# Attention softmax maxima turned by VectorE through DRAM instead of by TensorE, and two copies moved between engines

## The chip, the cores and the metric

The kernel runs on one core of a Trainium2 chip. The core has a matrix engine (PE in the profile, with a separate row PEld for its weight loads), a vector engine (VectorE, DVE), a scalar engine (ScalarE, ACT), GpSimd (POOL) and SyncE (SP), which here only issues transfers; ScalarE can issue transfers too. The engines work side by side and wait for each other by semaphores. PSUM is the memory that the matrix engine writes, in eight banks of 128 partitions by 512 fp32 numbers; SBUF is the large memory on chip; DRAM is outside. The metric is the time of one execution on the device in microseconds (us).

## The reference

One transformer block in fp32: layer norm, attention with 32 heads of width 20, output projection and residual, then layer norm, a gated feed-forward part and a second residual. S is 2048 tokens, D is 640, F is 1728.

```python
def _A_ref(x, wqkv, wo):
    qkv = (x @ wqkv).reshape(B, S, 3, H, Dh).transpose(2, 0, 3, 1, 4)
    q, k, v = qkv[0], qkv[1], qkv[2]
    scores = jnp.einsum("bhqd,bhkd->bhqk", q, k) * (Dh ** -0.5)
    p = _softmax(scores, axis=-1)
    o = jnp.einsum("bhqk,bhkd->bhqd", p, v)
    return o.transpose(0, 2, 1, 3).reshape(B, S, D) @ wo

def _B_ref(x, w_gate, w_up, w_down):
    return (_silu(x @ w_gate) * (x @ w_up)) @ w_down

h = x + _A_ref(_layernorm(x), A_wqkv, A_wo)
out = h + _B_ref(_layernorm(h), B_w_gate, B_w_up, B_w_down)
```

The softmax subtracts the maximum of each row of scores, one maximum for each head and query. That maximum is what the change is about.

## The kernel before

The kernel goes through three stages. In the first (up to the first score product, at 322.8 us) the inputs are normed and projected to queries, keys and values, and most maxima of the first units are worked out beside this. The second is attention proper (the last score product starts at 1468.4 us). The third is the projection of the attention's outputs and the feed-forward part.

**Units and steps.** Attention is cut into 32 units `u`: eight groups of four heads, and in each group four blocks of 512 queries (`g, c = divmod(u, 4)`). A unit takes 16 steps `kt`, one tile of 128 keys each, so there are 512 steps. In each step PE makes four score products (`scores`, L1182, its matmul is L1187), one for each head, keys by queries, into four PSUM banks that take turns. ScalarE takes the exponential out of the bank (L1193). The probabilities are then weighed with the values: `weigh` (L1195) makes four small matmuls for each step into one accumulator bank, `acc`, and it works on the step two back. There is only one accumulator, so a new unit's first weighing must wait until the last unit's sums have been copied out of it.

**Maxima.** The queries in SBUF, `q_stk`, hold for each pair of heads 60 rows of data and two rows more. These two rows (the *query rows* from here on) hold minus the maximum, split in a high and a low part so that no precision is lost in the matrix engine's rounded format (`F32R`); against rows of ones in the keys, the score product then comes out with the maximum taken away. So a unit's scores cannot begin before its query rows are written. The maxima come from products of their own with queries on the partitions: `max_one` (L240) makes one matmul of 128 queries by 512 keys in one of three PSUM banks (`ps_max`), and VectorE takes the maximum along the row (L250). Three of these go into every step, always for a later unit. When the last of a unit is done, `next_max` calls `max_all`: VectorE takes the maximum over the four blocks of keys and negates it, which leaves `neg`, 128 queries by 16 columns. Now the numbers stand along the partitions, but the query rows want them along a row, so they have to be turned. `max_finish` (L261) does this two steps later (`closing`): PE transposes them into one of the score banks, `split` (L87) rounds them to the high part on ScalarE and takes the rest on VectorE, and four transfers on SP bring them into the query rows.

**The order of a step** is written out by hand: `ORDER` holds the strings `"WsSmmSsM"` and `"WSsMMsSm"` for even and odd steps (`s`, `S` a score product, `m`, `M` a product for maxima, `W` the weighing with all that hangs on it: the turn of finished maxima, one task of the preparation of weights). Where no maxima remain, it is `"sSsSW"`. As the maxima run ahead evenly, the turn comes at different distances from the unit that needs it. In the kernel before, in units 2, 4, 6 and so on to 30 the turn stands nine steps ahead of the unit's first score, in units 5, 9, 13 and so on to 29 fifteen steps, and in units 1, 3, 7, 11, 15, 19, 23, 27 and 31 only four.

**What else runs beside it.** At the end of each unit `row_sums` (L1205) copies the whole accumulator with one ScalarE instruction (128x512) to SBUF and gathers the sums of the exponentials from it with small transfers; `reciprocals` writes one over them to DRAM (`r_d`), `spread` reads them back to all partitions (`rb`), and `store_o` multiplies and stores. `prepare_weights` (L988) works on the feed-forward part's weights, one task per step: a load on SP, sums on GpSimd, splits into high and low parts on GpSimd, and stores on SP (`store` in each task issues what the task before finished). `split_wo` (L883) splits the five pieces of the output weights late in the stage, the rounding on ScalarE and the rest on GpSimd. All transfers named here but the gathered sums of the last unit are issued by SP, in the order of the program; one that waits holds up those behind it. The same is true of each engine's own instructions.

Of the kernel before, what the change touches and what calls it, by code (L numbers as in the profile page):

```python
# [9 lines left out]
F32 = mybir.dt.float32  # L10
BF16 = mybir.dt.bfloat16
F32R = mybir.dt.float32r
I32 = mybir.dt.int32
AF = mybir.ActivationFunctionType
ALU = mybir.AluOpType
AX = mybir.AxisListType

P = 128
# [7 lines left out]
CH = 512  # L26
# [18 lines left out]
def tile_block(ctx: ExitStack, tc: tile.TileContext, x, wqkv, wo, wg, wu, wd, out):  # L45
# [10 lines left out]
    v_d = dram.tile([S, NG, VG], F32, name="v_d")  # L56
    o_d = dram.tile([D, S], F32, name="o_d")
    r_d = dram.tile([H, S], F32, name="r_d")
    z_d = [dram.tile([P, 2 * ND * CH], F32R, name=f"z_d{c}") for c in range(2)]
    t_d = [dram.tile([P, 8 * CH], F32R, name=f"t_d{i}") for i in range(2)]  # L60
    w_d = [dram.tile([P, 8, 4 * P], F32R, name=f"w_d{f}") for f in range(NF)]
# [191 lines left out]

    def max_all(u):

        ends[u] = stk.tile([P, G * TPC], F32, name="neg", tag="neg", bufs=2)
        nc.vector.tensor_reduce(
            ends[u], mxs[u].rearrange("p b h t k -> p (b h t) k"), axis=AX.X, op=ALU.max, negate=True
        )

    def max_finish(u):  # L261

        m = (ps_one if u else ps_max)()[: G * TPC, :P]
        nc.tensor.transpose(m, ends.pop(u), ident)
        parts = stk.tile([G * TPC, 2, P], F32R, name="m2", tag="m2", bufs=1)
        split(m, parts[:, 0], parts[:, 1], nc.vector)
        for b in range(2):
            for i in range(2):
                row = b * ROW + NPART + i
                first = b * 2 * TPC  # L270
                nc.sync.dma_start(
                    queries[u][row : row + 1].bitcast(F32).rearrange(
                        "r j (t p) -> r (j t) p", t=TPC
                    ),
                    parts[first : first + 2 * TPC, i, :].bitcast(F32),
                )
# [604 lines left out]
        nc.sync.dma_start(wo_raw[k], wo[k * P : (k + 1) * P, :])  # L881

    def split_wo(k):  # L883
        split(wo_raw.pop(k), wo_hi[:, k, :], wo_lo[:, k, :], nc.gpsimd)

    def projection(c, ps_of):

# [316 lines left out]

    def row_sums(acc, *queues):  # L1205
        o = pc.tile([P, CH], F32, name="o", bufs=1)
        nc.scalar.activation(o, acc, AF.Copy)  # L1207
        r = pc.tile([P, 16], F32, name="r")
        for j in range(G):
            queues[j % len(queues)].dma_start(  # L1210
                r[32 * j : 32 * j + 32, :],
                o[32 * j + DH : 32 * j + DH + 1, :].rearrange("r (p f) -> r p f", p=32),
            )
        return o, r
# [28 lines left out]
    def next_max(b):  # L1243
        if singles[b]:
            a = singles[b].pop(0)
            max_one(*a)
            left[a[0]] -= 1
            if left[a[0]] == 0:
                max_all(a[0])
                closing[a[0]] = now[0] + 2  # L1250

    def weigh_next():
        u, kt, probs = todo.pop(0)
# [9 lines left out]
    for u in range(NU):  # L1263
# [4 lines left out]
        for kt in range(NT):  # L1268
# [5 lines left out]
            for op in order:  # L1274
                if op in "mM":
                    next_max(int(op == "M"))
                elif op in "sS":
                    scores(u, kt, heads[op == "S"].pop(0), probs)
                else:
                    if len(todo) == 2:  # L1280
                        weigh_next()
                    for v in ready:
                        max_finish(v)
                    if extra:
                        extra.pop(0)()
                    if preparing and u and kt not in (3, 4):
                        preparing.pop(0)()
                    if now[0] == (NU - NC) * NT + 8:
                        unit_ring, last_ring = weight_rings()
                        unit_ring.fill()  # L1290
                        last_ring.fill()
# [603 lines left out]
```

## Time and profile before

| | |
|---|---|
| median of three runs | 2038.93 us (2038.71 to 2042.29) |
| the profiled execution | 2038.82 us, span of its trace 2037.0 us |
| PE busy | 2012.7 us, 99% of the span |
| PEld busy (overlaps PE) | 1249.9 us, 61% |
| VectorE busy | 1607.9 us, 79% |
| ScalarE busy | 1445.2 us, 71% |
| GpSimd busy | 774.1 us, 38% |
| exponentials, L1193 | 2048 on ScalarE, 614 ns each |
| maxima in attention, L250 | 1472 on VectorE, 684 ns each |
| score products, L1187 | 2048 on PE, 450 ns each |
| weighing, L1197 | 4096 on PE in the profile's count, 604 ns each |
| mean granted clock of PE | 0.999 |

The span begins with the first instruction and ends with the last; the execution's own time is a little longer. The ends of PE's matmuls are modelled and they overlap in its pipeline, so its busy share of 99% does not say that it is at its limit everywhere. In rows of the order of time the first number is the start in us from the span's beginning, the second the duration, then come the engine, the line of the kernel, the operation and the tile it writes and reads; a row with `x3` stands for three instructions in a run, and the brackets tell the idle time before it and what ended it. `SPq` rows are transfers as SP issues them, with the time it takes to issue.

### The profile page before, as it was taken

The page shows a single profiled execution, that of the slowest core. Times are in us where ns is not written, and L with a number is a line of the kernel's source. Part 1 is how long each engine was busy: PE and PEld are TensorE (multiplying, and loading weights), DVE is VectorE, ACT ScalarE, POOL GpSimd, SP SyncE. Part 2 cuts the span into 40 slices and gives each one's busy share as a digit, 9 for nine tenths or more (in the row PEclk, how much of TensorE's full clock was granted, in tenths as well). Part 3 has the DMA queues.
Part 4 walks back from the last instruction along what each step waited for, and adds up shares of the span by engine and source line. Part 5 has one row for each costly group of instructions (what it writes and reads, how often), then busy time and mean ns, then how long its engine had stood idle before and what let it go on. Part 6 is the DMA issues. An engine that isn't in the chain of part 4 may idle for free.

```text
span 2037.0 us, 40049 instructions
## 1 busy us (share of the span) xinstructions
PE 2012.7 (99%) x14322; PEld 1249.9 (61%) x14322; DVE 1607.9 (79%) x2826; ACT 1445.2 (71%) x2855; POOL 774.1 (38%) x1103
## 2 busy tenths in 40 slices
PE   8999999999999999999999999999999999999999
PEld 6989995343334333334333433345598888888888
DVE  5677778888888888888888888886378666676677
ACT  4677778999999999999999999987633222211221
POOL 6464423334342444352400011011146454754555
PEclk9999999999999999999999999999999999999999
DMA  7877563452634534435512131311158654974542
GB/s 244 255 244 260 175 206 89 116 161 79 187 104 124 166 115 143 149 127 176 156 46 79 27 94 44 92 62 55 33 184 302 220 192 157 344 273 158 202 150 94
DMA packets 194062, 310.01 MB, mean 152 GB/s; under 512 B 47760, under 2 KB 82576, under 8 KB 192840
## 3 DMA queue, kind: packets, MB, share of 16 engines
q1 hardware_dynamic: 187272, 283.85, 43.0%
q0 software_dynamic: 6496, 23.60, 4.0%
q8 instruction: 114, 1.87, 0.4%
q14 instruction: 84, 0.69, 0.1%
q10 hardware_dynamic: 96, 0.00, 0.0%
HBM read 207.75 MB, written 98.83 MB: 151 GB/s over the span
## 4 chain that ended last, share of the span: by engine, by line
PE 87%; DMA 3%; DVE 1%; issue 1%; POOL 1%; ACT 1%; SPq 1%; ACTq 0%; DVEq 0%; POOLq 0%
PE acc L1197 24%; PE ps_one L1187 16%; PE ps_a L1358 15%; PE ps_max L244 12%; PE ps_b L1452 8%; PE ps_one L568 6%; PE ps_max L211 2%; PE ps_max L918 2%; PE ps_b L918 1%; DMA units<-w_d 1%; DMA halves<-j_d 0%; DMA h<-in_A_x 0%; PE ps_max L953 0%; DVE tmp L1573 0%; ACT o L1207 0%
## 5 line engine op out<-in xcount | busy, mean ns | idle before, releaser
L1193 ACT ACTIVATE probs<-ps_one 128x512 f32<-128x512 f32 x2048 | 1056.7, 614 | 62.3 <-PE ps_one L1187 37.6
L250 DVE TENSOR_REDUCE mx<-ps_max 128x1 f32<-128x512 f32 x1472 | 926.2, 684 | 106.9 <-PE ps_one L1187 75.6
L1187 PE MATMUL ps_one<-q_stk,k_stk 62*128 62x512 f32 x2048 | 586.0, 450 | 2.8 <-DVE m L89 1.8
L1197 PE MATMUL acc<-probs,v_stk 128*32 128x512 f32 x4096 | 545.2, 604 | 0.0
L1187 PEld LDWEIGHTS ps_one<-q_stk,k_stk 62*128 62x128 f32 x2048 | 251.5, 184 | 432.7 <-ACT probs L1193 398.3
L244 PE MATMUL ps_max<-k_stk,q_stk 60*128 60x512 f32 x1472 | 381.2, 425 | 0.0
L244 PEld LDWEIGHTS ps_max<-k_stk,q_stk 60*128 60x128 f32 x1472 | 271.6, 186 | 24.1 <-DVE mx L250 0.9
L1573 DVE TENSOR_TENSOR tmp<-ps_a,tmp 128x512 f32<-128x512 f32 x208 | 141.2, 689 | 120.3 <-PE ps_a L1358 94.6
L233 DVE TENSOR_REDUCE mx<-ps_max 128x2 f32<-128x512 f32 x288 | 180.6, 685 | 66.5 <-PE ps_max L211 63.4
L1232 POOL TENSOR_TENSOR o<-o,rb 128x512 f32<-128x512 f32 x31 | 39.9, 1287 | 413.3 <-DMA q_stk<-q_d 241.5
L1197 PEld LDWEIGHTS acc<-probs,v_stk 128*32 128x32 f32 x4096 | 80.6, 108 | 174.8 <-issue 166.2
L223 ACT ACTIVATE ps_max<-ps_max 128x512 f32<-128x512 f32 x288 | 151.7, 583 | 47.5 <-PE ps_max L211 44.7
L1452 PE MATMUL ps_b<-halves,yp 128*128 128x320 f32 x1032 | 179.3, 308 | 2.0 <-DMA halves<-j_d 1.2
L1452 PEld LDWEIGHTS ps_b<-halves,yp 128*128 128x128 f32 x1032 | 165.1, 188 | 18.6 <-POOL yp L89 1.5
L1358 PE MATMUL ps_a<-t,units 128*128 128x512 f32 x624 | 162.6, 396 | 0.0
L1358 PE MATMUL ps_a<-z,units 128*128 128x512 f32 x516 | 133.9, 394 | 0.0
L89 POOL TENSOR_TENSOR yp<-y,yp 128x256 fp32r<-128x256 f32 x96 | 60.4, 629 | 188.2 <-ACT yp L88 188.2
L1358 PEld LDWEIGHTS ps_a<-t,units 128*128 128x128 f32 x624 | 112.6, 188 | 18.9 <-ACT tmp L1586 0.3
L1457 DVE TENSOR_TENSOR h<-ps_b,h 128x320 f32<-128x320 f32 x248 | 110.0, 481 | 6.9 <-PE ps_b L1452 5.4
L568 PE MATMUL ps_one<-z_hi,w_lo 64*128 64x512 f32 x380 | 113.7, 395 | 0.0
L568 PE MATMUL ps_one<-z_hi,w_hi 64*128 64x512 f32 x380 | 113.1, 396 | 0.0
L568 PE MATMUL ps_one<-z_lo,w_hi 64*128 64x512 f32 x380 | 111.7, 393 | 0.0
(211 smaller groups left out, 2643.3 us busy)
## 6 DMA issues: line engine op xcount, KB each, us to landing
units<-w_d SPq DMA_DIRECT2D x186, 256.0 KB
w_d<-stage SPq DMA_DIRECT2D x106, 256.0 KB
halves<-j_d SPq DMA_DIRECT2D x70, 320.0 KB
j_d<-stage SPq DMA_DIRECT2D x42, 320.0 KB
k_stk<-k_d SPq DMA_DIRECT2D x64, 160.0 KB
q_stk<-q_d SPq DMA_DIRECT2D x64, 160.0 KB
raw<-k_d SPq DMA_DIRECT2D x62, 160.0 KB
raw<-q_d SPq DMA_DIRECT2D x54, 160.0 KB
```

Of the source, the lines that this page charges most:

```text
L223: nc.scalar.activation(ps, ps, AF.Relu)
L233: nc.vector.tensor_reduce(mx[:, b, :, t, kc], ps.rearrange("p (j n) -> p j n", j=2), axis=AX.X, op=ALU.max,)
L244: nc.tensor.matmul(ps, queries[u][rows, pair, t * P : (t + 1) * P], keys[u // NC][rows, pair, kc * CH : (kc + 1) * CH], start=True, stop=True,
L250: nc.vector.tensor_reduce(mxs[u][:, b, pair, t, kc : kc + 1], ps, axis=AX.X, op=ALU.max)
L568: nc.tensor.matmul(ps, a[rows], b[rows], start=(i == n == 0), stop=(i == 1 and n == last), skip_group_check=True,)
L1187: nc.tensor.matmul(ps, keys[u // NC][rows, p, kt * P : (kt + 1) * P], queries[u][rows, p, :], start=True, stop=True,)
L1193: nc.scalar.activation(probs[p][:, b, :], ps, AF.Exp, scale=scale)
L1197: nc.tensor.matmul(acc[32 * j : 32 * j + 32, :], values[u // NC][:, kt, j * VW : j * VW + 32], probs[j // 2][:, j % 2, :], start=(kt == 0) ...
L1358: nc.tensor.matmul(ps.rearrange("p (t n) -> p t n", t=TPC), w[k][:, i], z[k][:, :, j], start=(first and m == 0), stop=(last and m == len(n ...
L1452: nc.tensor.matmul(ps, a, b, start=(n == 0), stop=(n == len(pairs) - 1))
L1457: nc.vector.tensor_tensor(out=h, in0=ps, in1=h, op=ALU.add)
L1573: add = lambda out, ps, x: nc.vector.tensor_tensor(out=out, in0=ps, in1=x, op=ALU.add)
```

## The change

Four things are changed.

1. *Maxima.* For every unit but the first, `max_all` now also splits the negated maxima into high and low parts, with two GpSimd instructions (a rounding copy and a subtraction), into one tile of 128 by 32. A new function `max_turn` takes the place of `max_finish` (which stays for unit 0): VectorE's own transpose turns the tile in blocks of 32 by 32, one transfer writes the result to a DRAM tile `m_d` (two of them take turns), and four transfers read it back, put together as rows, into the query rows. All five are on SP.
2. *When.* `closing` is set three steps after the last maximum instead of two.
3. *Row sums.* The accumulator is copied in two halves of 256 columns, one by ScalarE and one by VectorE.
4. *Output weights.* The rounding in `split_wo` goes from ScalarE to GpSimd, which does both instructions now.

The program built from it has two orders that the diff does not show: VectorE's half of the accumulator's copy waits for ScalarE's half, and the transpose waits for GpSimd's subtraction.

```diff
+    m_d = [dram.tile([P, 2 * G * TPC], F32, name=f"m_d{i}") for i in range(2)]
...
     def max_all(u):
-        ends[u] = stk.tile([P, G * TPC], F32, name="neg", tag="neg", bufs=2)
+        neg = ends[u] = stk.tile([P, G * TPC], F32, name="neg", tag="neg", bufs=2)
         nc.vector.tensor_reduce(
-            ends[u], mxs[u].rearrange("p b h t k -> p (b h t) k"), axis=AX.X, op=ALU.max, negate=True
+            neg, mxs[u].rearrange("p b h t k -> p (b h t) k"), axis=AX.X, op=ALU.max, negate=True
         )
+        if u:
+            both = ends[u] = stk.tile([P, 2, G * TPC], F32R, name="neg2", bufs=2)
+            nc.gpsimd.tensor_copy(both[:, 0], neg)
+            nc.gpsimd.tensor_tensor(
+                out=both[:, 1], in0=neg, in1=both[:, 0].bitcast(F32), op=ALU.subtract
+            )
+
+    def max_turn(u):
+        turned = stk.tile([P, 2 * G * TPC], F32, name="turned", bufs=2)
+        nc.vector.transpose(turned, ends.pop(u).bitcast(F32).rearrange("p i n -> p (i n)"))
+        nc.sync.dma_start(m_d[u % 2], turned)
+        n = 2 * TPC
+        rows = m_d[u % 2].rearrange("(q i r) c -> i r q c", q=4, i=2)
+        for b in range(2):
+            for i in range(2):
+                row = b * ROW + NPART + i
+                dst = queries[u][row : row + 1].bitcast(F32).rearrange("r j c -> r (j c)")
+                nc.sync.dma_start(dst, rows[i, b * n : (b + 1) * n])
 
     def max_finish(u):
-        m = (ps_one if u else ps_max)()[: G * TPC, :P]
+        m = ps_max()[: G * TPC, :P]
...
     def split_wo(k):
-        split(wo_raw.pop(k), wo_hi[:, k, :], wo_lo[:, k, :], nc.gpsimd)
+        raw = wo_raw.pop(k)
+        nc.gpsimd.tensor_copy(wo_hi[:, k, :], raw)
+        nc.gpsimd.tensor_tensor(
+            out=wo_lo[:, k, :], in0=raw, in1=wo_hi[:, k, :].bitcast(F32), op=ALU.subtract
+        )
...
     def row_sums(acc, *queues):
         o = pc.tile([P, CH], F32, name="o", bufs=1)
-        nc.scalar.activation(o, acc, AF.Copy)
+        half = CH // 2
+        nc.scalar.activation(o[:, :half], acc[:, :half], AF.Copy)
+        nc.vector.tensor_copy(o[:, half:], acc[:, half:])
...
-                closing[a[0]] = now[0] + 2
+                closing[a[0]] = now[0] + 3
...
                     for v in ready:
-                        max_finish(v)
+                        max_turn(v)
```

## The prediction

> **What bounds the kernel now.** I read the page first, for its span and its chain.
>
> ```profile
> span 2037.0 us, 40049 instructions
> ...
> PE 87%; DMA 3%; DVE 1%; issue 1%; POOL 1%; ACT 1%; SPq 1%; ACTq 0%; DVEq 0%; POOLq 0%
> ```
>
> All edits lie in the attention stage, 512 steps of one key tile each. PE carries 87% of the chain that ended last, so an edit is worth what it moves PE. The order of time in one stretch shows the two engines behind PE (start, duration, then the idle time before in brackets):
>
> ```profile
> 799.65 10.59 ACT L1193 ACTIVATE probs<-ps_one 128x512 f32<-128x512 f32 x20
> 804.15 1.89 DVE L250 TENSOR_REDUCE mx<-ps_max 128x1 f32<-128x512 f32 x3 [0.25 <-PE ps_one L1187]
> ```
>
> ScalarE looks full: twenty exponentials, five steps, in 10.59 us, nearly the 10.6 of PE's steps below. VectorE does three reductions in 1.89 us of each step and rests 0.25 us. How long a step is, and what each of the edited pieces costs PE, I take from the chain in order of time. Each row is the weighing of one step (start, duration), so the distance of two rows is one step of PE:
>
> ```profile
> 691.89 1.00 PE acc L1197 x8
> 694.01 0.99 PE acc L1197 x8
> 696.39 1.00 PE acc L1197 x8
> ...
> 707.00 0.99 PE acc L1197 x8
> 709.28 1.00 PE acc L1197 x8
> ...
> 715.66 1.00 PE acc L1197 x8
> 717.91 1.00 PE acc L1197 x8
> 720.28 0.99 PE acc L1197 x8
> ...
> 739.41 1.04 PE acc L1197 x8
> 742.26 1.00 PE acc L1197 x8
> ```
>
> A plain step is 2.12 us (691.89 to 694.01). Longer are the steps that the change touches: a turn of maxima through PE costs 0.26 (694.01 to 696.39) or, where it falls in an odd step, 0.25 + 0.13 = 0.38 over two steps (715.66 to 720.28); a copy of the row sums 0.16 (707.00 to 709.28); both together 0.73 (739.41 to 742.26), so 0.57 for that turn.
>
> **The change part by part.** First what goes away.
>
> Turns. Of the 31 turns in this stage, by the place of their step, 8 are of the 0.26 kind, 8 of the 0.38 kind, 7 of the 0.57 kind beside a row-sum copy, 7 more of the 0.38 kind, and the last lies in another stage (0.3): 2.1 + 3.0 + 4.0 + 2.7 + 0.3 = **-12.1 us**. PE loses its transpose, ScalarE and VectorE a small instruction each; nothing else covered them, so I take all of it.
>
> Now the prices of the rest:
>
> ```profile
> L1207 ACT ACTIVATE o<-acc 128x512 f32<-128x512 f32 x32 | 20.1, 628 | 1.0 <-issue 1.0
> L88 ACT ACTIVATE wo_hi<-wo_raw 128x640 fp32r<-128x640 f32 x5 | 4.4, 883 | 0.0
> L510 ACT ACTIVATE e<-ps_max 128x256 f32<-128x256 f32 x4 | 1.3, 382 | 0.5 <-PE ps_max L504 0.3
> L1473 DVE COPY own<-ps_b 128x320 f32<-128x320 f32 x32 | 14.2, 481 | 0.4 <-PE ps_b L1452 0.4
> L98 POOL TENSOR_TENSOR t_a<-r_a 128x4 f32<-128x4 f32 x9 | 1.8, 204 | 0.4
> ```
>
> Output weights. Five roundings leave ScalarE, 4.4 us. Not all of that reaches PE: of a row-sum copy's 0.63 it lost 0.16, a quarter, which would make 1.1. Between 1.1 and 4.4 I take 1.7, near the lower end, since the roundings too come singly between exponentials, but each is longer: **-1.7 us**. GpSimd takes them on when no weights are prepared any more.
>
> Row sums. Both halves read one accumulator, and in the changed program VectorE's half waits for ScalarE's half: they run one after the other. ScalarE's half is 0.38 (128x256), VectorE's about 0.41 (481 ns less a fifth of its columns). Together 0.79 against 0.63, so the accumulator comes free later, not sooner: the next weighing starts some 0.08 later. VectorE stands still until ScalarE is done and then copies, which puts its reductions back by about 0.3; its rest of 0.25 takes most of it back in the next step, but the third product of that step waits for the third buffer, about 0.18. So 0.26 takes the place of 0.16: +0.11 in 30 units, **+3.3 us**. Bounds: -0.15 each if both waits are hidden (-4.6), +0.3 each if the delay of VectorE reaches PE whole (+9). I am near the middle because the third buffer has no slack in the rows. [...] If the halves did run side by side, this term would be -4.6 and the sum about 2031.
>
> The split on GpSimd is two instructions of 0.2 (128x4) to 0.29: 0.4 us, hidden but for what stands behind it. The turn on VectorE I price between 0.16 and 0.28, the small VectorE instructions; it fits the rest of 0.25 and costs PE nothing. [...]
>
> The way through DRAM is the dear part. Rows of the DMA queue, for a write, the read that waits for it, and four small loads into the query rows:
>
> ```profile
> 715.19 0.61 SPq L1220 DMA_DIRECT2D r_d<-r  x1
> 717.20 0.58 SPq L1226 DMA_DIRECT2D rb<-r_d  x1
> ...
> 698.68 2.79 SPq L271 DMA_DIRECT2D q_stk<-m  x4
> ```
>
> From the start of a write to its reader is 2.0 us (715.19 to 717.20). The four reads are issued 0.7 apart, and the last is there another 2.0 after its issue by the same row: 2.0 + 2.1 + 2.0, about 6.0 us from write to use. For 22 units the turn comes 8 or 14 steps ahead of the first score: 17 us and more, nothing is lost. For the nine others (units 1, 3, 7, 11, ... 31) the turn is three steps ahead of its unit. Unit 3 stands for those whose queues are empty:
>
> ```profile
> 419.55 1.89 DVE L250 TENSOR_REDUCE mx<-ps_max 128x1 f32<-128x512 f32 x3
> ...
> 427.33 0.50 PE L1187 MATMUL ps_one<-q_stk,k_stk 62*128 62x512 f32 x2
> ```
>
> VectorE is free for the turn at 421.44, the write goes at 421.7, the rows are there at 427.7, and the first score is due at 427.33: 0.3 to 0.4 late, of which the first of two scores, whose rows come earlier, wins a little back. Units 1, 3, 7, 23, 27 at 0.3: **+1.5 us**; unit 31, whose turn stands behind other VectorE work, **+0.5**.
>
> Units 11, 15 and 19 are worse, since GpSimd is behind there and the queue in order:
>
> ```profile
> 697.57 0.74 POOL L1042 TENSOR_TENSOR sums<-raw,sums 128x256 f32<-128x256 f32 x1
> 698.73 0.72 POOL L1006 TENSOR_TENSOR stage<-raw,stage 128x256 fp32r<-128x256 f32 x1
> 701.57 0.39 SPq L996 DMA_DIRECT2D w_d<-stage  x1
> 702.01 0.42 SPq L168 DMA_DIRECT2D v_stk<-v_d  x1
> 703.69 0.50 PE L1187 MATMUL ps_one<-q_stk,k_stk 62*128 62x512 f32 x2
> ...
> 973.24 0.86 POOL L1101 TENSOR_TENSOR sums<-raw,sums 128x320 f32<-128x320 f32 x1
> 980.06 0.50 PE L1187 MATMUL ps_one<-q_stk,k_stk 62*128 62x512 f32 x2
> ```
>
> In unit 11's turn the split comes behind sums that end at 698.31, so VectorE (free at 697.80) waits for it until 698.7. The store of a weight piece and a load of values stand ahead of the maxima's write; the store needs the piece that ends at 699.45 before and 699.85 now. With 0.39 and 0.42 of issue the write goes at 700.7; with 0.3 behind the values' own packets the rows are there at 707.0, **3.3 late**. For unit 19 the same steps give: split from 974.10, its piece at 975.85, the write 976.7, the rows 983.0 against 980.06, 2.9 late. Units 11 and 19 are the first and the last of three; for unit 15, where GpSimd is a little less behind, I take 2.2. Together **+8.4 us**. PE stands still in this time and has no rest to make it up: its plain step is its own work.
>
> Sum: -12.1 - 1.7 + 3.3 + 1.5 + 0.5 + 8.4 = -0.1. The profiled execution took 2038.82 us (span 2037.0 and 1.8 around it), 0.1 under the median of 2038.93. I predict **2038.8 us**: gain and price cancel.
>
> **The rivals.** About 0.2% (4.1 us) is what a measurement of this kernel can tell from no change.
>
> (a) Slower: the way through DRAM is longer than its best row. The small reads and the write stand behind loads of values in just these steps (702.01), and 0.42 us is only their issue. If that costs 1.2 us more in each of the nine, which have no slack left, it is +10.8, 2049.6; it decides from 0.5 us in each. Against it: the pair quoted above, 2.0 us with other loads about it.
>
> (b) Slower: PE idles long enough at the late units to lose its clock. The busy times by stretch (start and end, PE's busy time second, the mean granted clock third from the end) show it once:
>
> ```profile
> 125.00:132.00 7.00, 5.12 (x41) 4.80 (x41) 5.33 (x8) 2.74 (x5) 2.63 (x4) 0.76 0.89 276
> 61.00:66.00 5.00, 2.61 (x45) 2.30 (x43) 4.86 (x7) 1.43 (x4) 3.28 (x5) 1.00 0.91 265
> ```
>
> After 1.9 us of idle PE (7.00 less 5.12) the mean granted clock of that stretch is 0.76, that is some 3.4 us at half speed, 1.7 us lost. Three late units: +5.1, 2043.9. [...] Against it: the stretch quoted second held an idle time of 2.4 us (5.00 less 2.61) at a mean clock of 1.00, so an idle time of this length does not decide it.
>
> (c) Faster: GpSimd isn't behind in units 11, 15, 19, because the queue ahead of it is emptied sooner without the old turn's waits. Then 8.4 falls to 1: 2031.4. Against it: GpSimd waits there for weight loads, which do not move.
>
> (d) Faster: the row-sum halves hide, -4.6 for +3.3: 2030.9.
>
> **How the numbers follow.** Cancelling within 0.2%: 0.40. Slower 0.35: (a) 0.15, (b) 0.08, and 0.12 for row sums at their upper bound of +9 (2044.5). Faster 0.25: (c) 0.13, (d) 0.12. The range takes in (a) to (d), 2029 to 2050; the likeliest case alone spans 2035 to 2043.
>
> **What would show it.** Right: no PE transpose in the steps that had one, those at 2.12; first scores of units 11, 15, 19 released by a DMA after two to three us of idle PE; row-sum steps still 0.2 to 0.3 long, with the copy on VectorE starting after ScalarE's. Wrong: first scores on time in all units, clean units over 1 us late, VectorE waiting for GpSimd elsewhere, or a granted clock under 1 in this stage.

## The result: 1.3% slower

The changed kernel takes 2068.69 us (median of four runs, 2066.18 to 2070.37), the kernel before 2039.05 beside it: a ratio of 1.0132, 95% interval 1.0118 to 1.0146. The prediction was 2038.8 us, with a range of 2029 to 2050; the measured time lies outside. The profiled execution took 2069.76 us.

Where the time went shows in the first lines of the changed kernel's page (compare them with the first fence of the prediction): PE's share of the chain that ended last fell from 87 to 77%, that of transfers rose from 3 to 8%.

```profile
span 2067.8 us, 40020 instructions
...
PE 77%; DMA 8%; DVE 2%; POOL 2%; SPq 2%; ACT 1%; issue 1%; ACTq 0%; DVEq 0%; POOLq 0%
...
L1211 PE MATMUL ps_one<-q_stk,k_stk 62*128 62x512 f32 x2048 | 584.7, 450 | 14.1 <-DMA q_stk<-m_d 12.3
L1221 PE MATMUL acc<-probs,v_stk 128*32 128x512 f32 x4096 | 552.4, 612 | 10.1 <-DVE o L1233 8.8
```

The last two lines are the score products and the weighing (L1187 and L1197 before). Behind the second bar stands how long PE was idle ahead of them: before the change 2.8 and 0.0 us, now 14.1, most of it until query rows come through DRAM, and 10.1, until VectorE has copied its half of the accumulator.

All of it lies in the attention stage. The summary of the score products' line gives the start of the first and of the last of the 2048; here for the kernel before, then for the changed one:

```profile
L1187 PE MATMUL ps_one<-q_stk,k_stk x2048: 383/492/522, 322.8 to 1468.4; 62*128 62x512 f32 x187
```

```profile
L1211 PE MATMUL ps_one<-q_stk,k_stk x2048: 383/492/792, 323.4 to 1498.0; 62*128 62x512 f32 x187
```

The stage grew from 1145.6 to 1174.6 us, by 29.0 of the 30.8 us that the span grew. Most steps became shorter all the same. The chain in order of time shows the same steps of units 11 and 12 that the prediction quoted:

```profile
731.53 1.00 PE acc L1221 x8
733.66 0.99 PE acc L1221 x8
735.92 0.99 PE acc L1221 x8
738.03 0.99 PE acc L1221 x8
...
757.17 1.04 PE acc L1221 x8
759.36 1.07 PE acc L1221 x8
761.58 1.06 PE acc L1221 x8
763.78 1.00 PE acc L1221 x8
```

A plain step is still 2.13 us (731.53 to 733.66). Two steps with a turn of the 0.38 kind took 4.62 and take 4.37 now (733.66 to 738.03): 0.25 is gone, but 0.13 of the 0.38 stays. The step with the turn beside a row-sum copy took 2.85; now the copy stretches three distances to 2.19, 2.22 and 2.20, which is 0.22 in all. Against these small gains stand about a dozen stalls.

**A stall in the second step of unit 6.** First SP's queue in the changed kernel, then the three engines:

```profile
517.14 0.34 SPq L272 DMA_DIRECT2D m_d<-turned  x1
521.05 2.80 SPq L279 DMA_DIRECT2D q_stk<-m_d  x4
...
530.71 2.75 SPq L1261 DMA_DIRECT2D o_d<-o  x4
```

```profile
537.72 0.38 ACT L1232 ACTIVATE o<-acc 128x256 f32<-128x256 f32 x1 [3.50 <-DMA k_stk<-k_d]
538.14 0.42 DVE L1233 COPY o<-acc 128x256 f32<-128x256 f32 x1 [3.86 <-ACT o L1232]
538.62 1.08 PE L1221 MATMUL acc<-probs,v_stk 128*32 128x512 f32 x4 [3.66 <-DVE o L1233]
```

Unit 6's maxima are turned eight steps ahead, so nobody needs them yet. But the reads stand right behind their write in the queue and wait for it 3.9 us (517.14 to 521.05), and everything behind them waits too: loads of keys, stores and loads of weights, and the stores of `o`, the tile that takes the accumulator's copy. Those go at 530.71, against 526.92 before. There is one such tile, so the next copy out of the accumulator must wait until they have landed. The bracket at ScalarE's half names a load of keys; the chain, in order of time, has that load end at 533.17 us and names the stores of `o` as the last thing ahead of the copy:

```profile
533.19 4.00 DMA o_d<-o
```

ScalarE's half waits 3.5 us, VectorE's half behind it, and PE stands still for 3.66 us. In the kernel before the same copy had no idle time ahead of it. Units 10 and 18 show the same (3.42 and 1.69 us). Unit 2 loses less and by another way from the same queue: the small transfers that gather the row sums come late, VectorE waits 1.14 us for them, and its reductions stand behind. All waits of SP for this one thing, from its list of waits in the stage (us in total, times, longest):

```profile
SPq L279 <- DMA m_d<-turned: 82.5, 31, 5.4
```

**A late first score, unit 11.** VectorE, SP's queue and PE of the changed kernel:

```profile
710.48 0.21 DVE L271 STREAM_TRANSPOSE turned<-neg 128x32 f32<-128x32 f32 x1 [1.07 <-POOL neg L264]
711.62 0.35 SPq L1020 DMA_DIRECT2D w_d<-stage  x1
712.01 0.43 SPq L169 DMA_DIRECT2D v_stk<-v_d  x1
712.55 0.52 SPq L272 DMA_DIRECT2D m_d<-turned  x1
715.40 2.81 SPq L279 DMA_DIRECT2D q_stk<-m_d  x4
718.28 0.76 PE L1211 MATMUL ps_one<-q_stk,k_stk 62*128 62x512 f32 x1 [2.15 <-DMA q_stk<-m_d]
```

This is the chain that the prediction drew: VectorE waits for the split, the write for a weight store and a load of values, the first score for the rows. PE is idle 2.15 us and then 0.60 more until the second pair of rows is there, 2.75 where 3.3 was predicted. What comes next was not in the sum. By stretch, with the mean granted clock third from the end:

```profile
715.00:718.00 3.00, 1.13 (x9) 0.16 (x8) 1.59 (x3) 1.54 (x4) 2.84 (x6) 1.00 0.02 3
718.00:721.00 3.00, 2.12 (x7) 1.18 (x7) 0.53 (x1) 1.16 (x3) 1.87 (x4) 0.54 0.58 183
721.00:724.00 3.00, 3.00 (x14) 1.02 (x14) 1.68 (x4) 1.49 (x5) 0.00 (x0) 0.50 0.70 235
```

The clock falls to half for 6.8 us, and the steps that follow take 4.8 and 3.0 us in place of 2.13. It fell six times in this stage, in units 6, 10, 11, 15, 19 and 23, five times for 6.83 us and once for 3.41.

Taken together, by the distance of first scores from step to step against the same step where it does not stall (2.26 and 2.22 us for the two steps of a row-sum copy): units 2, 6, 10 and 18 lose 0.9, 6.1, 5.8 and 1.6 (14.4 us), units 11, 15 and 19 lose 6.4, 6.9 and 6.9 (20.2), units 3, 7 and 23 lose 0.2, 0.6 and 3.3 (4.1). That is 38.7 us in stalls. PE's idle times of over 0.5 us add up to 21.7; nearly all the rest, some 17 us, is work at half clock. (The clock was at half for 37.5 us in this stage, of which PE was busy 31.7; half of that is 15.9.)

### The profile page after: what moved, and what is told of

It is laid out like the page before. It is cut to its first block, busy times and chain, and to the rows that moved or that the text cites. A ratio compares the mean times of both kernels' runs of the same rounds, so it can differ in the third digit from the quotient of the medians.

```text
span 2067.8 us, 40020 instructions
## 1 busy us (share of the span) xinstructions
PE 2019.6 (98%) x14291; PEld 1256.0 (61%) x14291; DVE 1615.6 (78%) x2858; ACT 1436.0 (69%) x2819; POOL 791.8 (38%) x1170
## 4 chain that ended last, share of the span: by engine, by line
PE 77%; DMA 8%; DVE 2%; POOL 2%; SPq 2%; ACT 1%; issue 1%; ACTq 0%; DVEq 0%; POOLq 0%
PE acc L1221 20%; PE ps_a L1384 15%; PE ps_one L1211 12%; PE ps_max L245 10%; PE ps_b L1478 8%; PE ps_one L588 6%; PE ps_max L212 2%; PE ps_max L942 2%; PE ps_b L942 2%; DMA m_d<-turned 2%; DMA k_stk<-k_d 2%; DMA rb<-r_d 1%; SPq L279 1%; DVE mx L251 1%; DMA raw<-in_B_w_down 1%
## 5 line engine op out<-in xcount | busy, mean ns | idle before, releaser
L1211 PE MATMUL ps_one<-q_stk,k_stk 62*128 62x512 f32 x2048 | 584.7, 450 | 14.1 <-DMA q_stk<-m_d 12.3
L1221 PE MATMUL acc<-probs,v_stk 128*32 128x512 f32 x4096 | 552.4, 612 | 10.1 <-DVE o L1233 8.8
L263 POOL CAST neg<-neg 128x16 fp32r<-128x16 f32 x31 | 6.5, 209 | 293.4 <-DVE neg L258 293.4
```

The costliest lines, as they stand in the source:

```text
L1211: nc.tensor.matmul(ps, keys[u // NC][rows, p, kt * P : (kt + 1) * P], queries[u][rows, p, :], start=True, stop=True,)
L1221: nc.tensor.matmul(acc[32 * j : 32 * j + 32, :], values[u // NC][:, kt, j * VW : j * VW + 32], probs[j // 2][:, j % 2, :], start=(kt == 0) ...
```

## The experiments

Each kernel ran beside the kernel before on the same chip, whose median lay between 2039 and 2042 us; so what counts is the distance to it. For the changed kernel that is +29.6 us.

**The accumulator copied whole again.**

```diff
-        nc.scalar.activation(o[:, :half], acc[:, :half], AF.Copy)
-        nc.vector.tensor_copy(o[:, half:], acc[:, half:])
+        nc.scalar.activation(o, acc, AF.Copy)
```

> The changed kernel with the accumulator copied whole by ScalarE again, as before the change. Theory (the tile o comes free late, because the stores that empty it stand behind the maxima's reads in SP's queue): ScalarE's copy waits for the same tile, so PE stands still in the second steps of units 6, 10 and 18 as long as in the changed kernel (3.7, 3.4 and 1.7 us), and only the halves' own price goes, 30 x 0.07 = 2 us: 2066 to 2068. Rival (VectorE's half, which the trace names as what ends these waits, is their cause): the three stalls go and 13.5 us with them: 2055.

Measured: 2066.37 us, +24.8 (ratio 1.0118, 1.0101 to 1.0135). That is 4.8 us less than the changed kernel where some 2 were expected, but the two intervals overlap. The stalls stay, now with ScalarE's whole copy as what ends them:

```profile
L1221 PE MATMUL acc<-probs,v_stk 128*32 128x512 f32 x4096 | 549.4, 609 | 9.4 <-ACT o L1231 9.3
```

PE's idle time ahead of the weighing is 9.4 us where it was 10.1, with 4.9, 2.1 and 2.3 us in units 6, 10 and 18. So VectorE's half, which the trace of the changed kernel names, is only the last link; the cause lies ahead of both halves.

**Two tiles for the copy.**

```diff
-        o = pc.tile([P, CH], F32, name="o", bufs=1)
+        o = pc.tile([P, CH], F32, name="o")
```

> The changed kernel with two buffers for the tile o that takes the accumulator's copy, in place of one. Theory (o comes free late): the three stalls in the second steps of units 6, 10 and 18 go, with the clock that they cost, 6.1 + 5.8 + 1.6 = 13.5 us: 2055, give or take 2, while the reads of the maxima still wait 2.8 to 4 us for their write. Rival (VectorE's half is the cause): no change, 2068.7.

Measured: 2058.34 us, +16.8 (ratio 1.0084, 1.0068 to 1.0099): 12.8 less than with one tile.

```profile
L1221 PE MATMUL acc<-probs,v_stk 128*32 128x512 f32 x4096 | 548.9, 608 | 1.5
L245 PE MATMUL ps_max<-k_stk,q_stk 60*128 60x512 f32 x1472 | 376.9, 427 | 3.2 <-DVE mx L251 2.9
```

```profile
685.41 0.25 DVE L1244 RECIPROCAL r<-r 128x16 f32<-128x16 f32 x1 [3.21 <-DMA r<-o]
686.26 1.09 PE L245 MATMUL ps_max<-k_stk,q_stk 60*128 60x512 f32 x2 [1.99 <-DVE mx L251]
```

The idle time ahead of the weighing is gone (1.5 us), so it is the tile that came free late. A part comes back in another place: in unit 10 the row sums themselves, which SP fetches with small transfers, arrive late; VectorE waits 3.21 us for them with its reductions behind it, and PE 1.99 us for a buffer. The queue is as late as before, only the first to suffer is another.

**Reads issued later.** For the units with a turn 8 or 14 steps ahead, the four reads go out three steps after the write.

```diff
         nc.sync.dma_start(m_d[u % 2], turned)
+
+    def max_read(u):
...
                         max_turn(v)
+                        reading[v] = now[0] + (0 if v * NT - now[0] < 4 else 3)
+                    for v in [v for v, at in reading.items() if at == now[0]]:
+                        max_read(v)
```

> The changed kernel, but where a turn is 8 or 14 steps ahead of its unit the four reads are issued three steps after the write instead of right behind it, so that SP's queue doesn't stand still for the way through DRAM. Units with the short margin are left as they are. Theory (that standstill of 2.8 to 4 us is what makes the stores of o late): the stalls of units 6, 10 and 18 go as with two buffers, 2055, give or take 2. Rival (o's stores are late for another reason, the loads of keys or the weights): 2067 to 2069. The late units 11, 15, 19 and 23 stay as they are in both.

Measured: 2053.93 us, +12.4 (ratio 1.0062, 1.0045 to 1.0078). With one tile `o` as in the changed kernel, no stall is left in units 2, 6, 10's second step and 18's second step, and PE waits 1.4 us in all ahead of the weighing:

```profile
L1214 PE MATMUL ps_one<-q_stk,k_stk 62*128 62x512 f32 x2048 | 580.4, 447 | 12.8 <-DMA q_stk<-m_d 11.9
L1224 PE MATMUL acc<-probs,v_stk 128*32 128x512 f32 x4096 | 546.9, 606 | 1.4
```

The reads' wait in SP's queue is the cause of that group of stalls. What is left is the first line: late first scores.

**Units with a short margin turned by PE.**

```diff
-        if u:
+        if u and not short(u):
...
+    def short(u):
+
+        return u == 1 or u % NC == 3
...
-        m = ps_max()[: G * TPC, :P]
+        m = (ps_one if u else ps_max)()[: G * TPC, :P]
...
-                closing[a[0]] = now[0] + 3
+                closing[a[0]] = now[0] + (2 if short(a[0]) else 3)
...
-                        max_turn(v)
+                        (max_finish if short(v) else max_turn)(v)
```

> The changed kernel, but the nine units whose turn is only three steps ahead (1, 3, 7, 11 and so on to 31) have their maxima turned by PE two steps after the last maximum as before the change; the other 22 go through DRAM. Theory (the way through DRAM makes just these units late): first scores of units 3, 7, 11, 15, 19 and 23 on time, 25.4 us less, nine PE turns back at 0.38 each, +3.4: 2046.7, give or take 3, with the stalls in the second steps of units 6, 10 and 18 unchanged. Rival (those units are late because GpSimd or SP are late in these steps whatever is asked of them): PE still waits over 1 us at the first scores of 11, 15 and 19, 2056 or more.

Measured: 2047.75 us, +6.2 (ratio 1.0028, 1.0017 to 1.0039).

```profile
L1215 PE MATMUL ps_one<-q_stk,k_stk 62*128 62x512 f32 x2048 | 579.7, 448 | 1.0 <-ACT probs L1221 0.8
L1225 PE MATMUL acc<-probs,v_stk 128*32 128x512 f32 x4096 | 547.9, 607 | 10.8 <-DVE o L1237 9.3
```

The mirror image of the run before: first scores are on time (1.0 us), the stalls ahead of the weighing stay (10.8, with 1.1 us in unit 14 too, where the changed kernel has none). Two separate faults, then, and the 38.7 us are their sum.

**Products for PE to do while it waits.** On the kernel with later reads.

```diff
+            if kt == 0:
+                for _ in range({11: 9, 15: 15, 19: 8, 23: 4}.get(u, 0)):
+                    nc.tensor.matmul(ps_max(), queries[u][:NPART, 0, :P],
+                                     keys[g][:NPART, 0, :CH], start=True, stop=True)
```

> The kernel with later reads, with extra products on PE ahead of the first scores of units 11, 15, 19 and 23 (9, 15, 8 and 4 of the maxima's products once more, into the maxima's banks, not read by anyone), so that PE works where it would wait for the query rows. Theory (an idle time of over 2 us costs PE its clock, and that is a good part of what a late unit costs): the steps after the stalls of units 11 and 15 are back at 2.1 to 2.3 us with a granted clock of 1.00, and some 4.4 us go (1.9 and 2.6): 8 us above the kernel before, in place of 12.4. Rival (the steps after the stall are long because the second half of the query rows is late, not because of the clock): they stay at 2.8 to 4.9 us, 12 to 14 above.

Measured: 2047.82 us, +7.0 (ratio 1.0037, 1.0023 to 1.0052), against +12.4 without the extra products. By the medians that is 5.4 us less, near the 4.4 of the clock theory, but the two intervals overlap, and the profile does not show the gain: its stage is 1156.5 us, without the extra products 1153.6. It was taken of the slowest of the five executions (2053.65), and there unit 15 kept its clock while unit 11 lost it with the extra products running:

```profile
703.00:714.00 11.00, 10.64 (x45) 4.29 (x43) 4.40 (x8) 4.13 (x8) 5.92 (x12) 0.69 0.43 132
844.00:857.00 13.00, 12.52 (x72) 5.87 (x65) 7.29 (x12) 7.76 (x16) 3.51 (x6) 1.00 0.51 154
```

In unit 15 the two steps behind the stall are 2.58 and 2.12 us, in place of 4.82 and 2.16 without the extra products. In unit 11 PE had no longer gap than 0.3 us, and its clock fell all the same. So work in the gap kept the clock in one unit and not in another; that it saves time rests on the medians alone, and idle time alone does not say when the clock falls.

**A load of values out of the write's way.** On the kernel with later reads.

```diff
-                load_values(g + 1, (kt - 8) // 2 * TPC, (kt - 6) // 2 * TPC)
+                for at in {12: (), 14: (12, 14)}.get(kt, (kt,)):
+                    load_values(g + 1, (at - 8) // 2 * TPC, (at - 6) // 2 * TPC)
```

> The kernel with later reads, with the third load of values of each group issued one and a half steps later, together with the fourth, so that it doesn't stand right ahead of the maxima's write in units 11, 15, 19 and 23. Theory (the write waits for its packets behind those of that load and of the stores): from the write to its first read 2.0 to 3.0 us in units 11, 15 and 19 in place of 2.9, 4.0 and 2.6, some 2 to 5 us less: 8 to 10 us above the kernel before. Rival (the interval is set by something else, for example another transfer or the write's own length): unchanged within 0.3 us, 12.4 above.

Measured: 2047.0 us, +6.1 (ratio 1.0035, 1.002 to 1.0049), 6.2 less than with the load in place. From the write to its first read: 1.8 us in unit 11 (699.51 to 701.29 below), 3.5 in unit 15 and 2.0 in unit 19, against 2.9, 4.0 and 2.6. In unit 23 it stayed at 3.1 us. PE's idle times ahead of the first of the late scores are 0.5, 3.2 and 0.9 us in units 11, 15 and 19, against 2.2, 3.7 and 2.0.

```profile
699.51 0.38 SPq L272 DMA_DIRECT2D m_d<-turned  x1
701.29 2.79 SPq L282 DMA_DIRECT2D q_stk<-m_d  x4
```

So the write did wait for the load issued ahead of it, by 1.1, 0.5 and 0.6 us in units 11, 15 and 19, though unit 23 must have another reason (the last section has it).

**Both remedies: the short units on PE, later reads for the others.** The edits of two runs above put together; where they meet:

```diff
-                        max_turn(v)
+                        if short(v):
+                            max_finish(v)
+                            continue
+                        max_turn(v)
+                        reading[v] = now[0] + 3
+                    for v in [v for v, at in reading.items() if at == now[0]]:
+                        max_read(v)
```

> Both remedies at once: units 1, 3, 7, 11 and so on turned by PE as before the change, the others through DRAM with reads three steps after the write; row sums in halves and roundings on GpSimd as in the changed kernel. Theory (the stalls are all that is wrong with the way through DRAM): no idle time of PE over 0.5 us at a first score or a first weighing, and the stage is 8.6 us shorter than before the change: 2032 to 2034 against 2039 to 2041.6, ratio 0.9955 to 0.997. Rival (something else of the change costs as well): at or above the kernel before.

Measured: 2034.34 us, 6.5 below the kernel before (ratio 0.9969, 0.9959 to 0.998). No idle time of PE over 0.5 us at a first score or a first weighing, but for the first step, where the kernel before has it too. The stage is 1139.9 us, 5.7 shorter than before the change, where 8.6 was expected; two steps of unit 30 in which the clock was at half make 1.3 of the difference.

**The same with the accumulator copied whole.**

```diff
-        half = CH // 2
-        nc.scalar.activation(o[:, :half], acc[:, :half], AF.Copy)
-        nc.vector.tensor_copy(o[:, half:], acc[:, half:])
+        nc.scalar.activation(o, acc, AF.Copy)
```

> The same with the accumulator copied whole by ScalarE. Theory (the halves run one after the other and cost 0.08 us in each of 30 units): 2.4 us less than with the halves, 11 below the kernel before, ratio 0.994 to 0.996. Rival (the halves relieve ScalarE and gain elsewhere): equal or slower than with the halves.

Measured: 2034.64 us (ratio 0.9967, 0.9954 to 0.998). The medians are equal, so the 2.4 us that the theory expected do not show in the time; in the profiles the stage is 4.0 us shorter than with the halves, of which 1.3 are the two steps of unit 30. A row-sum copy costs 0.15 us here and 0.22 in halves.

**The row sums alone.** The kernel before with the halves.

```diff
-        nc.scalar.activation(o, acc, AF.Copy)
+        half = CH // 2
+        nc.scalar.activation(o[:, :half], acc[:, :half], AF.Copy)
+        nc.vector.tensor_copy(o[:, half:], acc[:, half:])
```

> The kernel before with one edit: the accumulator copied in two halves. Theory (VectorE's half follows ScalarE's): a row-sum copy stretches two steps by 0.14 and 0.09 us in place of one by 0.15, +0.08 in each of 30 units, 2.4 us above the kernel before, which is at the edge of what the runs can tell; the steps of the trace show it. Rival (the halves take load off ScalarE): equal or below, and steps of under 2.27 us.

Measured: 2043.07 us against 2041.92 (ratio 1.0006, 0.9996 to 1.0016): nothing that these runs can tell from no change. The weighings of one copy:

```profile
706.08 0.91 PE acc L1197 x5
708.27 1.06 PE acc L1197 x8
710.49 1.06 PE acc L1197 x8
712.68 1.00 PE acc L1197 x8
```

2.19, 2.22 and 2.19: 0.22 over three distances, where one step of 2.28 held the whole copy before. So the theory holds by the steps, 0.07 to 0.08 us in most units. Beside a turn on PE it did not: those units' two long steps are 2.33 and 2.61 us with the halves and 2.34 and 2.64 without. The stage is 0.7 us longer, not 2.4.

**The output weights alone.** The kernel before with the roundings on GpSimd.

```diff
-        split(wo_raw.pop(k), wo_hi[:, k, :], wo_lo[:, k, :], nc.gpsimd)
+        raw = wo_raw.pop(k)
+        nc.gpsimd.tensor_copy(wo_hi[:, k, :], raw)
+        nc.gpsimd.tensor_tensor(
+            out=wo_lo[:, k, :], in0=raw, in1=wo_hi[:, k, :].bitcast(F32), op=ALU.subtract
+        )
```

> The kernel before with one edit: the roundings of the output weights on GpSimd. Theory: the five steps of 2.40 to 2.65 us in units 25 to 27 fall to 2.12 and their like, 1.9 us less. Rival (GpSimd is late and the first product that needs the weights waits): a stall behind the last unit, or no change.

Measured: 2038.98 us, 2.9 below the median of the kernel before beside it (ratio 0.9982, 0.9973 to 0.9992). The five long steps are gone: in units 25 to 27 the steps of 2.40 to 2.65 us are 2.12 to 2.13 now, or 2.47 where a turn stands, and together 1.9 us shorter. (The stage of the profiled execution is 1146.7 us all the same, because its clock fell for 6.8 us in unit 0.)

**The split of three units on VectorE.** On the kernel with later reads.

```diff
+            engine = nc.vector if u in (11, 15, 19) else nc.gpsimd
-            nc.gpsimd.tensor_copy(both[:, 0], neg)
-            nc.gpsimd.tensor_tensor(
+            engine.tensor_copy(both[:, 0], neg)
+            engine.tensor_tensor(
```

> The kernel with later reads, with the split of the maxima of units 11, 15 and 19 on VectorE in place of GpSimd. Theory (in these units the write is held by SP's queue more than by the split: stores that wait for GpSimd, and loads, stand ahead of it): the transpose goes about 0.5 to 1 us sooner, but the write at most 0.4 us sooner, and PE still stands still 1.5 to 3.7 us at the first scores of 11, 15 and 19. Rival (waiting for GpSimd's split is what makes them late): idle times under 1 us.

Measured, in one execution: 2052.68 us. Idle times at the first scores: 2.2, 2.8 and 0.7 us in units 11, 15 and 19, where the kernel with later reads had 2.2, 3.7 and 2.0. Against the moment at which PE comes to the first score, the write goes 0.2 us later in unit 11, but 0.8 and 1.2 sooner in 15 and 19, partly because the step that holds the split grew from 2.13 to 2.4 and, in unit 18, to 3.0 us, so that PE comes later. The theory holds for unit 11; for 15 and 19 it had the split too small.

**Two steps in place of three for the short units.** On the kernel with later reads.

```diff
-                closing[a[0]] = now[0] + 3
+                closing[a[0]] = now[0] + (2 if a[0] % NC == 3 else 3)
...
-                        reading[v] = now[0] + (0 if v * NT - now[0] < 4 else 3)
+                        reading[v] = now[0] + (0 if v * NT - now[0] < 5 else 3)
```

The second pair of lines keeps the reads of these units right behind their write.

> The kernel with later reads, but in units 3, 7, 11 and so on the turn comes two steps after the last maximum in place of three. Theory (margin decides where the queues are empty; SP's queue decides in 11, 15 and 19): units 3, 7 and 23 on time (0.1, 0.7 and 1.5 us less), the turn's write in units 11 and 15 at most 1 us sooner relative to the first score, with idle times of over 1 us left there. Rival (the third step is what makes all of them late): no idle time over 0.5 us at any first score.

Measured, in one execution: 2042.11 us. My theory missed here: every first score is on time, also in units 11, 15 and 19. Counted from the first score of unit 10, the write of unit 11 went 1.7 us sooner (29.7 against 31.5) and its first read 3.2 (31.2 against 34.4), because both now stand ahead of the weight store and the load of values. But the wait moved:

```profile
696.68 0.22 POOL L264 TENSOR_TENSOR neg<-neg,neg 128x16 fp32r<-128x16 f32 x1
696.94 0.21 DVE L271 STREAM_TRANSPOSE turned<-neg 128x32 f32<-128x32 f32 x1 [3.30 <-POOL neg L264]
697.18 0.35 SPq L272 DMA_DIRECT2D m_d<-turned  x1
697.78 1.39 PE L245 MATMUL ps_max<-k_stk,q_stk 60*128 60x512 f32 x2 [2.06 <-DVE mx L251]
```

VectorE stands 3.3 us waiting for GpSimd's split, its reductions stand behind the transpose, and PE waits 2.06 us for a buffer that they free; the clock falls again (a weight load for these products takes 0.28 us behind the wait and 0.19 ahead of it). With three steps this wait was 1.07 us and hidden.

**Two steps, and the split of units 11, 15 and 19 on VectorE: all units through DRAM.** On the kernel with later reads, with the reads of the short units as in the run above (not shown again).

```diff
-            nc.gpsimd.tensor_copy(both[:, 0], neg)
-            nc.gpsimd.tensor_tensor(
+            engine = nc.vector if u in (11, 15, 19) else nc.gpsimd
+            engine.tensor_copy(both[:, 0], neg)
+            engine.tensor_tensor(
...
-                closing[a[0]] = now[0] + 3
+                closing[a[0]] = now[0] + (2 if a[0] % NC == 3 else 3)
```

> The kernel with later reads, units 3, 7, 11 and so on turned two steps after the last maximum, and the split of units 11, 15 and 19 on VectorE: all units through DRAM. Theory (the place in SP's queue that the third step costs and VectorE's wait for GpSimd's split, together, are the whole of what made these units late): no idle time of PE over 0.5 us in the stage after its first step, the stage 1134 to 1138 us long, ratio to the kernel before 0.994 to 0.997. Rival (something else holds units 11, 15 and 19, or the reads): idle times over 0.5 us remain there, stage above 1140.

Measured: 2033.62 us, 7.4 below the kernel before (ratio 0.9967, 0.9954 to 0.998). One idle time over 0.5 us is left after the first step, 0.84 at unit 15's first score; the clock stays at 1.00 through the stage (no score product takes over 523 ns, where half clock made it 792 in the changed kernel), and PE is idle 1.8 us in all ahead of the 2048 score products. The stage is 1138.7 us, just above the expected 1134 to 1138. So the third step, with the place in SP's queue that it costs, and VectorE's wait for the split are nearly the whole cause of the late units; these runs do not part the lost step itself from the place in the queue. Unit 15 is held by the queue once more, as the order of its rows shows: its turned maxima are ready at 832.58 us, but a store of weights stands ahead of their write, waits 4.7 us for GpSimd and goes at 833.96, four stores of `o` follow, and the write goes at 835.99.

**The same with the accumulator copied whole.**

```diff
-        half = CH // 2
-        nc.scalar.activation(o[:, :half], acc[:, :half], AF.Copy)
-        nc.vector.tensor_copy(o[:, half:], acc[:, half:])
+        nc.scalar.activation(o, acc, AF.Copy)
```

> The same with the accumulator copied whole by ScalarE. Theory (halves cost 0.08 us per unit): the stage 2.4 us shorter, 1132 to 1135 us, ratio 0.993 to 0.996. Rival: equal or longer than with the halves.

Measured: 2032.9 us, 8.1 below the kernel before (ratio 0.9955, 0.9938 to 0.9972), the lowest ratio of all, though its interval overlaps those of the run before it and of the two versions with the short units on PE. The stage is 1137.2 us, 1.5 shorter than with the halves where 2.4 was expected; its clock fell once, in unit 0, which made one step 1.0 us longer.

## Why the prediction was wrong, step by step

| term | predicted | measured |
|---|---|---|
| turns leave PE | -12.1 | -10.0 |
| output weights | -1.7 | -1.9 |
| row sums in halves | +3.3 | +2.3 |
| units 1, 3, 7, 23, 27 late | +1.5 | +4.1 |
| unit 31 late | +0.5 | 0 |
| units 11, 15, 19 late | +8.4 | +20.2 |
| SP held up (units 2, 6, 10, 18) | 0 | +14.4 |
| sum | -0.1 | +29.1 |

The measured column is from the distances of the steps in the two traces; the stage grew by 29.0.

*Right in kind and near in size.* The two gains and the row sums. The turns were 2 us too dear in the sum, because 0.13 of each 0.38 belongs to `max_all`, whose reduction on VectorE stays: the step of 2.26 us (733.66 to 735.92) shows it in the changed kernel, with no turn in it. VectorE's half does follow ScalarE's: in the rows above it starts at 538.14 us, when the other, begun at 537.72, has run its 0.38. Of its 32 copies 29 waited for ScalarE's, 21.8 us in all; no run here shows the two side by side. GpSimd and VectorE did the split and the transpose at the prices taken (0.20 and 0.22, and 0.20).

*The step that failed first* is "For 22 units the turn comes 8 or 14 steps ahead of the first score: 17 us and more, nothing is lost." It asked only when the rows are needed, and not what stands behind the reads in SP's queue while they wait for their write. That wait was 82.5 us in all. In four units what stood behind it was needed: 14.4 us, shown by two tiles for `o`, which hide most of it, and by later reads, which take it away. The old turn had four transfers on SP as well, but nothing in it waited for a transfer of its own.

*The second* is the price of a late unit. How late the rows come was right within a third: PE was idle 2.75, 4.43 and 3.56 us in units 11, 15 and 19, 10.7 in all against 8.4. But 20.2 were lost: the other 9.5 are the clock, which the prediction had as a rival for 0.08 and at 1.7 us each. What spoke against it, one idle time of 2.4 us at full clock, was a single row from a stage of other work. The clock fell in all three units and in units 6, 10 and 23 too, mostly for 6.83 us and not for 3.4. It fell in unit 11 after PE had been idle for 2.15 us, and in unit 23 after 0.68 and 1.04.

*The third* is the way through DRAM itself, rival (a). 2.0 us from write to read was right where nothing else moved (units 5, 17 and 25: 1.6 us), but it was 2.9 to 4.0 in the late units and 3.7 to 6.1 in the units that are turned behind loads of queries and keys. The load of values ahead of it accounts for 0.5 to 1.2 us of that in units 11, 15 and 19, and in unit 23 a packet of the instruction queue for most of it (the last section).

GpSimd's lag and the order of SP's queue in units 11, 15 and 19 were right as causes: with the turn one step sooner the split becomes the wait, with the split on VectorE the queue remains, and with both edits the units are on time but for 0.84 us in one.

Not settled: what decides whether an idle time costs the clock. In one run it fell with no gap over 0.3 us; 1.69 us in unit 18 of the changed kernel cost none; and the idle time of some 0.8 us in unit 0, which every version has, cost it in three runs (the accumulator copied whole again, the output weights alone, and the last one) and not in the others.

## What to carry to other kernels

A wait for a transfer's own predecessor belongs on no queue that others stand in: put steps of other work between a write and the read that waits for it, or everything issued behind them inherits the round trip, here 82.5 us of SP's time in 31 waits. When a part leaves a critical engine for a longer way round, price the longer way for the units with the least margin and for the queues it passes, because that is where the gain of all others is lost. And look at the granted clock behind each stall: here stalls of 21.7 us in all cost some 17 more in clock, though not each of them did.

## What the runs showed of the hardware that was not expected

In six of ten profiles a write of 16 KB was finished late, behind a transfer that no instruction of the kernel issues. In unit 23 of the changed kernel the write goes out at 1142.97 us with nothing of the kernel's ahead of it, and its reader at 1146.54. The transfers' view from 1143 to 1147, in 40 slices of 0.1 us (busy tenths, then GB/s):

```profile
DMA  0000000054000005000000001000000000000000
GB/s 0 0 0 0 0 0 0 0 86 63 5 0 0 0 0 164 0 0 0 0 0 0 0 0 6 4 0 0 0 0 0 0 0 0 0 0 0 0 0 0
...
q8 instruction: 1, 0.02, 1.4%
```

Most of the write moves at 1143.8 to 1144.1. At 1144.5 a single packet of the instruction queue moves (16 KB, 0.92 us by its record), and the last eight packets of the write follow only at 1145.4, when it is through. The reader comes 1.0 us after that. In unit 27, without such a packet, the reader came 1.43 us after the write. That the one packet held the eight back is read from their order, and the other runs bear it out. Ten of the profiles have this write of unit 23. In six a packet of the instruction queue moves 0.9 to 1.6 us after the write is issued; there the last eight packets of the write come 0.9 to 1.5 us behind the others, and the reader 3.1 to 3.7 us after the write. In the other four (the extra products, the two steps, and the last two versions) there is no such packet, the write moves in one go, and the reader comes 1.4 to 1.5 us after it.
